# B and C of chunks 4 and 5 before the last w_in quarter, and units 0 and 1 in turn on the first three quarters

## The chip, the cores and the metric

The kernel runs on one core of a Trainium2 chip. A core has a matrix engine (TensorE, PE in the profile), a vector engine (VectorE, DVE), an activation engine (ScalarE, ACT), a general engine (GpSimd, POOL) and a queue engine that issues most DMAs (SyncE, SP). Each takes its instructions in the order in which they are written, and waits at the first one whose operands are not there. The metric is device time in microseconds, the median of the runs. Lower is better.

## The reference

A selective state-space layer, followed by a feed-forward layer with gelu. Sizes: 4 batches, 8 heads, 768 positions, head size 32, state size 16; then 3072 tokens of width 256 through 2048 and back.

```python
x, a, B, C = ...                       # x (4,8,768,32), a (4,8,768), B and C (4,8,768,16)
for c in range(nc):                    # chunks of 32
    la = log(clip(a, 1e-6, 1))[chunk]; cum = cumsum(la)
    M = (C @ B^T) * exp(cum_i - cum_j) * causal
    y = M @ x + (C @ state) * exp(cum)
    state = exp(sum(la)) * state + sum_j B_j x_j exp(cum_last - cum_j)
h = y.reshape(3072, 256) @ w_in        # w_in (256, 2048)
out = gelu_tanh(h) @ w_out             # w_out (2048, 256), out float32
```

## The kernel before

The positions are cut into chunks of 128, six to a batch, 24 in all. Two chunks make a unit, so units 0 to 2 are batch 0, 3 to 5 batch 1 and so on. Decays are products of `a`, found by one scan per batch on VectorE; B is multiplied by the decay product of its position and C divided by it, so that no mask of exponentials is needed.

The steps of a unit `u`, by the names used in the program, are these. `G.u` is the Gram product of C and B on TensorE, into two pairs of PSUM banks, `ga` and `gb`. `M.u.0` and `M.u.1` multiply it with the causal mask on VectorE, once for `ga` and once for `gb`. `D.u` gives the state sums of its two chunks; `S.u.k` adds one to the running state on VectorE, and `SP.c` spreads the state of chunk `c` over the heads. `Y.u` multiplies mask product and spread state with x and C on TensorE (`Yi` and `YI` for units 4 and up, two units together), and `yev.u` copies the result to `xm`, the input of the feed-forward layer. `s1.u.i` is a part of `xm @ w_in` into one PSUM bank, `gelu.u.i` reads that bank on ScalarE, `s2.u.k.q` is a quarter of `gelu @ w_out` for chunk `2u + k`, `oev` copies the sum out and `store` writes it. For units 0 to 3, `s1` has eight parts of four matmuls of 256 columns, and a part needs w_in's quarter `i // 2`; `s2` has four quarters per chunk, each four matmuls of 256 columns. So a part of `s1` and a quarter of `s2` are the same amount of work on TensorE.

Batch 0 is treated apart, so that work starts early. Its first four chunks have loads of their own (`load_bc0`, `load_x4`), and a scan over the first 128 positions (`clipq`, `Rq`). Chunks 4 and 5 (unit 2) have others: `load_bc1` brings their B and C, `load_a` brings all of `a`, and `clip`, `R`, `tp2`, `recip1` on VectorE give their decays; `mul1`, `T1`, `bh1`, `ce1`, `N1`, `bn1` turn B and C for them, and `pe`, `pp`, `pend` find the decays of whole chunks. Batch 1 is turned on TensorE (`mul`, `T`, `E`, `N`, `bn`, `F`), batches 2 and 3 through DRAM: `load_wr` writes the products, `load_tr` and `load_bn` read them back turned. `G.6`, the first of batch 2, waits for these.

The weights come as four quarters of w_in (`load_wi`, 512 KB each) and four of w_out (`load_wo`), in float32, and are cast to bfloat16 in halves by `wi.q.k` and `wo.q.k`, mostly on GpSimd. `load_x.u` and `castx.u` do the same for x from unit 2 on.

There are four single PSUM banks, `bank_a`, `bank_b`, `bank_o` and `bank_y`. A step takes a bank by default (`s1` and `D` take a and b in turn, `s2` takes o, `Y` takes y), or the one named behind an `@` in the table. Before the first work TensorE multiplies zeros into `bank_y`: `~47` means 47 blocks of 128 columns of that filler.

The order of everything is written out by hand: the string `ORDERED` lists the steps, and each is issued when its name comes. `name:A`, `:D`, `:P` or `:S` puts it on another engine than its default one. An engine therefore sees its own steps in the order of the list, and every wait is on data, on a buffer or on a bank. DMAs rotate through eight completion semaphores, so a DMA is issued when the eighth one before it has landed.

Of the kernel before, what the change touches and what calls it, by code (L numbers as in the profile page):

```python
# [21 lines left out]
load_wi.2 SP.0 ~13 Y.0 wi.0.1:A wi.0.0:A S.0.0 clip R S.0.1 yev.0.0.2 wi.1.1 XX.1 XD.1 wi.1.0 tp2 wi.2.1
xn.2 s1.0.0 G.1 S.1.0 s1.0.1 xn.3 gelu.0.0 gelu.0.1 s1.0.2 gelu.0.2 M.1.1 wi.2.0 M.1.0 s1.0.3 gelu.0.3
s1.0.4 s1.0.5 recip1 S.1.1 gelu.0.4 gelu.0.5 SP.1 load_wi.3 wi.3.1 wi.3.0 load_bc1.1 s1.0.6 load_bc1.0
mul1.0:P SP.2 pe mul1.1:P T1.0 bh1:D tp6 Y.1 gelu.0.6 pp load_wo.0 pend:D yev.1.0.2 T1.1 N1 wo.0.0 s1.0.7
load_x.2 ce1.1:D castx.2.None ce1.0:D recip.1 s1.1.0 bn1 SP.3 gelu.0.7 wo.0.1 G.2 D.2 gelu.1.0 S.2.0
s1.1.1 gelu.1.1 s2.0.0.0 s1.1.2 gelu.1.2 s1.1.3 load_bc.1.1 SP.4 load_bc.1.0 M.2.1 M.2.0 gelu.1.3
load_wo.1 s2.0.1.0 mul.1.0 s1.1.4 hold.4 mul.1.1:P recip.2 load_x.3 gelu.1.4 wo.1.0 s1.1.5 wo.1.1 Y.2
gelu.1.5 castx.3.None s1.1.6 yev.2.0.2 T.1.0 s1.1.7 gelu.1.6 load_wo.2 E.1.0 T.1.1 s1.2.0 N.1 gelu.1.7
# [1053 lines left out]
```

## Time and profile before

| | |
|---|---|
| median of 3 runs | 116.78 us (116.25 to 117.2) |
| the profiled execution, its span | 116.7 us |
| TensorE busy (matmuls) | 107.8 us, 92% |
| VectorE, ScalarE, GpSimd busy | 66.2, 69.8, 24.8 us |
| granted TensorE clock | full in all 40 slices |
| DMA | 15.99 MB, 137 GB/s over the span |
| longest wait of TensorE on another engine after the start | 1.3 us, for the casts of w_in |

The page of a profile gives no other time of its execution than the span, from the first to the last instruction. In the lines shown below, L and a number is the line of the kernel; L790 is `s1` of units 0 to 3, L816 `s2`, L644 and L637 `G`, L679 `D`, L701 and L710 `Y`, L721 `Yi`, L654 `M`, L752 `S`, L759 `SP`, L801 `gelu`. Lines 348, 350 and 352 are a copy or cast on ScalarE, GpSimd and VectorE, whatever the step. A line of the order in time is start, length, engine, line, operation, tiles and count; in square brackets stands how long the engine had been idle, and what ended that.

### The profile page before, as it was taken

To read this page: it belongs to the slowest core of one execution; us is meant where nothing else is said; L and a number is where in the kernel's file an instruction comes from. 1 tells how busy PE (TensorE), PEld (TensorE's weight loads), DVE (VectorE), ACT (ScalarE), POOL (GpSimd) and SP (SyncE) were. 2 spreads that over 40 slices of the span, in tenths; PEclk is the share of its full clock that TensorE was granted. 3 is DMA by queue.
4 is the path that set the end of the run, shared out by engine and by line. 5 is a ranking of instruction groups with operands and counts; after the bars stand their busy time and mean duration, and the time that the engine had idled before them with its cause. 6 is when DMAs were issued, how large, how long until landed. Compare 5 with 4: busy or idle time off the path is not lost.

```text
span 116.7 us, 3120 instructions
## 1 busy us (share of the span) xinstructions
PE 107.8 (92%) x1276; PEld 77.6 (66%) x1284; DVE 66.2 (57%) x136; ACT 69.8 (60%) x135; POOL 24.8 (21%) x53
## 2 busy tenths in 40 slices
PE   6989758799999999999999999999999999999990
PEld 2345547588788969665766775777657676777870
DVE  3799995699899279399806901928614521011010
ACT  4179675587575655469774688834775565763500
POOL 7644737455526400050010200000000000000000
PEclk9999999999999999999999999999999999999999
DMA  0999949996997787895978802220000013301032
GB/s 26 254 313 314 305 81 239 286 230 178 296 249 117 144 168 152 201 248 170 217 145 142 169 3 93 96 90 6 0 0 0 0 51 123 101 0 45 6 135 90
DMA packets 43102, 15.99 MB, mean 137 GB/s; under 512 B 36688, under 2 KB 41552, under 8 KB 43088
## 3 DMA queue, kind: packets, MB, share of 16 engines
q1 hardware_dynamic: 42992, 15.76, 54.9%
q8 instruction: 10, 0.16, 0.7%
q10 hardware_dynamic: 96, 0.03, 0.1%
q14 instruction: 4, 0.03, 0.1%
HBM read 11.07 MB, written 3.93 MB: 129 GB/s over the span
## 4 chain that ended last, share of the span: by engine, by line
PE 52%; SPq 27%; DMA 14%; issue 2%; ACT 2%; DVE 0%; DVEq 0%
PE bank_y L816 13%; PE bank_o L816 12%; SPq L175 10%; PE bank_b L795 8%; SPq L194 7%; PE bank_a L795 6%; DMA wf<-in_moe_w_in_dram 5%; SPq L168 5%; DMA x_t<-in_x_dram 4%; PE bank_o L795 3%; DMA scr<-bc 2%; DMA bn<-scr 2%; PE bank_y L795 2%; PE bank_b L816 2%; PE bank_a L816 1%
## 5 line engine op out<-in xcount | busy, mean ns | idle before, releaser
L816 PEld LDWEIGHTS <-gT 128*128 128x128 bf16 x384 | 37.1, 98 | 10.4 <-issue 0.6
L816 PE MATMUL bank_o<-w_out_sb,gT 128*128 128x256 bf16 x192 | 26.1, 273 | 0.0
L816 PE MATMUL bank_y<-w_out_sb,gT 128*128 128x256 bf16 x160 | 21.2, 273 | 0.1
L795 PEld LDWEIGHTS <-w_in_sb 128*128 128x128 bf16 x128 | 14.2, 114 | 7.5 <-issue 0.4
L804 ACT ACTIVATE gT<-bank_b 128x512 bf16<-128x512 f32 x25 | 14.9, 597 | 6.5 <-PE bank_b L795 6.1
L654 DVE TENSOR_TENSOR m<-ga,tri 128x1024 bf16<-128x1024 f32 x12 | 14.6, 1218 | 5.2 <-PE gb L637 5.2
L804 ACT ACTIVATE gT<-bank_a 128x512 bf16<-128x512 f32 x21 | 12.6, 599 | 6.8 <-PE bank_a L795 2.5
L790 PEld LDWEIGHTS <-w_in_sb 128*128 128x128 bf16 x128 | 13.5, 114 | 4.1 <-POOL w_in_sb L350 1.6
L801 ACT ACTIVATE gT<-bank_b 128x512 bf16<-128x512 f32 x17 | 10.1, 597 | 8.7 <-PE bank_b L790 8.6
L795 PE MATMUL bank_b<-xm,w_in_sb 128*128 128x512 bf16 x48 | 14.5, 380 | 0.2
L654 DVE TENSOR_TENSOR m<-gb,tri 128x1024 bf16<-128x1024 f32 x11 | 13.4, 1216 | 0.0
L790 PE MATMUL bank_b<-xm,w_in_sb 128*128 128x256 bf16 x68 | 10.3, 274 | 1.7 <-POOL w_in_sb L350 1.3
L795 PE MATMUL bank_a<-xm,w_in_sb 128*128 128x512 bf16 x36 | 11.2, 380 | 0.1
L352 DVE COPY o_sb<-bank_y 128x256 f32<-128x256 f32 x5 | 2.1, 425 | 15.7 <-PE bank_y L816 13.7
L801 ACT ACTIVATE gT<-bank_a 128x512 bf16<-128x512 f32 x15 | 8.9, 595 | 3.4 <-PE bank_a L790 3.3
L790 PE MATMUL bank_a<-xm,w_in_sb 128*128 128x256 bf16 x60 | 9.0, 273 | 0.9 <-ACT gT L801 0.4
L759 DVE SCALAR_TENSOR_TENSOR sp_new<-s_new,pend,bmask 128x256 bf16<-128x256 f32 x17 | 8.2, 497 | 0.3 <-DVE s_new L752 0.2
L352 DVE CAST xm<-bank_a 128x512 bf16<-128x512 f32 x4 | 2.8, 692 | 9.7 <-PE bank_a L734 9.7
L773 PE MATMUL bank_y<-wz 128*128 128x512 bf16 (+2 forms) x20 | 7.1, 499 | 1.1 <-DVE warm L225 1.1
L510 POOL TENSOR_TENSOR bc<-bc_t,pt 128x768 bf16<-128x768 f32 x3 | 4.7, 1563 | 14.6 <-PE bank_o L795 11.6
L804 ACT ACTIVATE gT<-bank_o 128x512 bf16<-128x512 f32 x10 | 6.0, 597 | 2.4 <-PE bank_o L795 2.3
L348 ACT ACTIVATE xm<-bank_y 128x512 bf16<-128x512 f32 x8 | 4.8, 596 | 3.8 <-PE bank_a L734 3.5
(149 smaller groups left out, 130.9 us busy)
## 6 DMA issues: line engine op xcount, KB each, us to landing
out_dram<-o_sb SPq DMA_DIRECT2D x24, 128.0 KB, 1.8
x_t<-in_x_dram SPq DMA_DIRECT2D x20, 128.0 KB, 4.3
wf<-in_moe_w_in_dram SPq DMA_DIRECT2D x4, 512.0 KB, 6.4
wf<-in_moe_w_out_dram SPq DMA_DIRECT2D x4, 512.0 KB, 6.5
bc_t<-in_C_dram SPq DMA_DIRECT2D x3, 384.0 KB, 6.9
bc_t<-in_B_dram SPq DMA_DIRECT2D x3, 384.0 KB, 6.3
scr<-bc SPq DMA_DIRECT2D x4, 192.0 KB, 3.0
x_t<-in_x_dram SPq DMA_DIRECT2D x1, 512.0 KB, 5.0
```

The source lines that it names most:

```text
L168: nc.sync.dma_start(out=d["bc"][:, i], in_=(B, C)[i][b].rearrange("h (p r) n -> p h (r n)", r=R6))
L175: (nc.scalar if eng == "ACT" else nc.sync).dma_start(out=XF[u][:, k], in_=x[b, :, (c + k) * Q:(c + k + 1) * Q, :].rearrange("h p d -> p h d"))
L194: nc.sync.dma_start(out=WF[("o", q)], in_=wo[q])
L352: nc.vector.tensor_copy(out=o, in_=i)
L654: nc.vector.tensor_tensor(out=m_of(u)[:, 2 * i:2 * i + 2].rearrange("p g k e t -> p (g k e) t"), in0=gx[i].rearrange("p g (k t) -> p (g k) ...
L759: nc.vector.scalar_tensor_tensor(out=sp_new.rearrange("p (g d) -> p g d", g=4), in0=(XN[0][:, H * D:H * D + 64] if gc == 0 else state[("s" ...
L773: nc.tensor.matmul(out=t[:, 0:m * 128], lhsT=wz, rhs=w3.to_broadcast([128, m, 128]), start=True, stop=True, skip_group_check=True)
L790: nc.tensor.matmul(out=hp[:, j * T:(j + 1) * T], lhsT=w_in_k[:, w, q, k], rhs=xm[:, w, u * T:(u + 1) * T], start=(w == 0), stop=(w == 1))
L795: nc.tensor.matmul(out=hp, lhsT=w_in_k[:, w, q, k], rhs=xm[:, w, u * T:u * T + PT], start=(w == 0), stop=(w == 1))
L801: nc.scalar.activation(gts[u][:, 2 * i:2 * i + 2], hp.rearrange("p (j t) -> p j t", j=2), AF.Gelu_apprx_tanh)
L804: nc.scalar.activation(gts[("p", u)][:, i], hp, AF.Gelu_apprx_tanh)
L816: nc.tensor.matmul(out=ops[gc], lhsT=gts[u][:, fi, k * Q:(k + 1) * Q], rhs=w_out_sb[:, fi, :], start=(fi == 0 and (u > 0 or k == 0)), stop ...
```

## The change

Only the table changes. Three things are moved.

First, the DMA issues on SP's queue, in the stretch from the first w_in quarter to x of unit 4. The order before is this (`bcf_95` is B and C of chunks 4 and 5, `bc_t` those of batch 1, `wf` the weights, `x_t` x of a unit):

```order
L190 DMA wf<-in_moe_w_in_dram 128x2x512
L162 DMA a_t<-in_a_dram 32x256 x3
L162 DMA a_t<-in_a_dram 32x192
L190 DMA wf<-in_moe_w_in_dram 128x2x512 x3
L154 DMA bcf_95<-in_C_dram 128x8x32
L154 DMA bcf_95<-in_B_dram 128x8x32
L194 DMA wf<-in_moe_w_out_dram 128x1024
L175 DMA x_t<-in_x_dram 128x8x32 x2
L168 DMA bc_t<-in_C_dram 128x8x96
L168 DMA bc_t<-in_B_dram 128x8x96
L194 DMA wf<-in_moe_w_out_dram 128x1024
L175 DMA x_t<-in_x_dram 128x8x32 x2
```

The same stretch of SP's queue after the change (line numbers are one higher):

```order
L191 DMA wf<-in_moe_w_in_dram 128x2x512 x3
L163 DMA a_t<-in_a_dram 32x256 x3
L163 DMA a_t<-in_a_dram 32x192
L155 DMA bcf_95<-in_B_dram 128x8x32
L155 DMA bcf_95<-in_C_dram 128x8x32
L191 DMA wf<-in_moe_w_in_dram 128x2x512
L195 DMA wf<-in_moe_w_out_dram 128x1024
L176 DMA x_t<-in_x_dram 128x8x32 x2
L195 DMA wf<-in_moe_w_out_dram 128x1024
L169 DMA bc_t<-in_C_dram 128x8x96
L169 DMA bc_t<-in_B_dram 128x8x96
L195 DMA wf<-in_moe_w_out_dram 128x1024
```

The second and third w_in quarter now stand ahead of `a`, B and C of chunks 4 and 5 ahead of the fourth, and each of the next w_out quarters one place earlier among the small loads.

Second, the parts of `s1`. ScalarE's evictions show it, since each `gelu` reads the bank of one part (`gT`), and `xm` is the eviction of a `Y`. ScalarE before, from unit 0's second x to unit 1's second part:

```order
L348 ACTIVATE x16_393<-bank_o_145 128x256
L801 ACTIVATE gT_395<-bank_b_144 128x2x256
L801 ACTIVATE gT_395<-bank_a_143 128x2x256
L801 ACTIVATE gT_395<-bank_b_144 128x2x256
L801 ACTIVATE gT_395<-bank_a_143 128x2x256
L801 ACTIVATE gT_395<-bank_b_144 128x2x256
L801 ACTIVATE gT_395<-bank_a_143 128x2x256
L801 ACTIVATE gT_395<-bank_b_144 128x2x256
L348 ACTIVATE xm_140<-bank_y_146 128x2x2x128
L348 ACTIVATE bn01_136<-ga_141 128x256
L801 ACTIVATE gT_395<-bank_b_144 128x2x256
L801 ACTIVATE gT_395<-bank_a_143 128x2x256 x2
```

ScalarE after, from the same place to the sixth part of unit 0 and the first four of unit 1:

```order
L349 ACTIVATE x16_395<-bank_o_145 128x256
L802 ACTIVATE gT_403<-bank_b_144 128x2x256
L802 ACTIVATE gT_403<-bank_y_146 128x2x256
L802 ACTIVATE gT_403<-bank_a_143 128x2x256
L802 ACTIVATE gT_403<-bank_o_145 128x2x256
L802 ACTIVATE gT_403<-bank_b_144 128x2x256
L349 ACTIVATE xm_140<-bank_y_146 128x2x2x128
L802 ACTIVATE gT_403<-bank_a_143 128x2x256
L802 ACTIVATE gT_403<-bank_o_145 128x2x256
L802 ACTIVATE gT_403<-bank_b_144 128x2x256
L802 ACTIVATE gT_403<-bank_y_146 128x2x256
L802 ACTIVATE gT_403<-bank_a_143 128x2x256
```

The parts go round all four banks, and behind six parts of unit 0 come four of unit 1, ahead of the two of unit 0 that need the fourth quarter. On TensorE the order is now 0.0 to 0.4, `Y.1`, 0.5, 1.0 to 1.2, `T1.0`, 1.3, `T1.1`, `N1`, 0.6, 0.7, `G.2`, `pp`, 1.4, 1.5, `s2.0.0.0`, `D.2`.

Third, the steps up to `G.5` are newly ordered on every engine. `G.1` comes before `Y.0`; on VectorE `M.1.1` and `M.1.0` come ahead of `clip` and the scan; more `s2` work comes before `G.3`, `G.4` and `G.5`; `D.2` takes bank y and `D.4` bank a; w_out's casts are all on GpSimd, and one half of w_in's fourth quarter on VectorE. The filler before `Y.0` is 4 blocks, not 13. VectorE near unit 5, before (`x_t_776` is x of unit 6, `x_t_773` of unit 5, `m_862` the mask product of unit 4, `m_929` of unit 5):

```order
L654 TENSOR_TENSOR m_862<-gb_142,tri_112 128x1024
L654 TENSOR_TENSOR m_862<-ga_141,tri_112 128x1024
L352 CAST x16_896<-x_t_776 128x512
L352 CAST x16_919<-x_t_773 128x512
L654 TENSOR_TENSOR m_929<-gb_142,tri_112 128x1024
L752 SCALAR_TENSOR_TENSOR s_new_940<-s_new_858,pend_129,bank_a_143 128x64
```

And after (`x_t_808` is x of unit 5, `x_t_811` of unit 6, `m_884` unit 4, `m_941` unit 5):

```order
L655 TENSOR_TENSOR m_884<-gb_142,tri_112 128x1024
L655 TENSOR_TENSOR m_884<-ga_141,tri_112 128x1024
L353 CAST x16_931<-x_t_808 128x512
L655 TENSOR_TENSOR m_941<-gb_142,tri_112 128x1024
L353 CAST x16_943<-x_t_811 128x512
L753 SCALAR_TENSOR_TENSOR s_new_950<-s_new_880,pend_129,bank_a_143 128x64
```

Unit 5's x is cast first, and unit 6's cast stands between the two halves of unit 5's mask product. From `D.5` on, the steps stand in the order of before, but for `s2.2.1.0` to `s2.2.1.2`, which now come ahead of `G.5`. Of the table itself, two pieces of the beginning:

```diff
-c_warm c_sel c_cz c_bmask clipq load_wi.0 load_a.0:S load_a.1:S load_a.2:S load_a.3:S Rq tpq recip0 c_m16
+c_m4 c_warm c_sel c_cz c_bmask clipq load_wi.0 Rq tpq recip0 c_m16 mulc.0 ~47 tw.1 ew.1.1:A mulc.1 tw.2
...
-load_wi.2 SP.0 ~13 Y.0 wi.0.1:A wi.0.0:A S.0.0 clip R S.0.1 yev.0.0.2 wi.1.1 XX.1 XD.1 wi.1.0 tp2 wi.2.1
+xn.1 ME.3 xn.0:D SP.0 S.0.0 ~4 G.1 Y.0 load_bc1.0 load_bc1.1 wi.0.1:A wi.0.0:A yev.0.0.2 M.1.1 XX.1 XD.1
```

93 lines of the change are left out of this document (47 added, 46 removed).

## The prediction

> **What bounds the kernel now.** I read the page's busy shares first, then busy time by stretch, what TensorE waited for, and the order in time of TensorE, VectorE, GpSimd and the DMA issues. First the page, and two stretches:
>
> ```profile
> PE 107.8 (92%) x1276; PEld 77.6 (66%) x1284; DVE 66.2 (57%) x136; ACT 69.8 (60%) x135; POOL 24.8 (21%) x53
> 10.00:22.00 12.00, 8.77 (x163) 6.10 (x160) 9.51 (x27) 8.28 (x17) 6.54 (x12) 1.00 0.90 239
> 60.00:70.00 10.00, 9.75 (x135) 7.05 (x134) 4.92 (x10) 6.25 (x13) 0.62 (x1) 1.00 0.62 119
> ```
>
> After the length of a stretch come TensorE (matmul, weight load), VectorE, ScalarE, GpSimd, granted clock, DMA share and GB/s. From 60 us TensorE is full (9.75 of 10). From 10 to 22 us it is busy 8.77 of 12, the ends of pipelined matmuls included. So the end moves by what the first 22 us give and what the rest doesn't give back. Matmuls of that stretch, in time (start, length), and one piece of the chain of waits:
>
> ```profile
> 12.16 0.60 PE L790 MATMUL bank_b<-xm,w_in_sb 128*128 128x256 bf16 x4 [0.41 <-DVE s_new L752]
> 17.87 0.63 PE L790 MATMUL bank_b<-xm,w_in_sb 128*128 128x256 bf16 x4 [1.31 <-POOL w_in_sb L350]
> 21.91 0.21 PE L679 MATMUL bank_b<-x,bn 128*32 128x64 bf16 x4 [0.73 <-POOL x L350]
> 22.06 0.63 PE L790 MATMUL bank_a<-xm,w_in_sb 128*128 128x256 bf16 x4
> 43.12 1.31 PE bank_y L816 x12
> ```
>
> The last row gives the unit of account: 12 matmuls in 1.31 us, so a group of four (an `s1` step of units 0 to 3, or an `s2` step) holds TensorE 0.437 us. From 12.16 to 22.06 us it did nine groups, 3.9 us of work, beside the small steps. It waits because `s1` alternates between two banks, because all eight groups of unit 0 stand before unit 1, and because the last two of them need the fourth w_in quarter (1.31 us, until 17.87).
>
> **The first 22 us.** GpSimd's casts of the second and third quarter, and what `a` takes ahead of them:
>
> ```profile
> 12.31 1.17 POOL L350 CAST w_in_sb<-wf 128x512 bf16<-128x512 f32 x2 [1.94 <-DMA wf<-in_moe_w_in_dram]
> 13.63 1.18 POOL L350 CAST w_in_sb<-wf 128x512 bf16<-128x512 f32 x2 [0.16 <-DMA wf<-in_moe_w_in_dram]
> 8.00:10.00 2.00, 1.95 (x54) 1.26 (x47) 1.96 (x4) 1.83 (x5) 1.64 (x8) 1.00 0.95 279
> a_t<-in_a_dram SPq DMA_DIRECT2D x3, 32.0 KB, 4.9
> ```
>
> The four pieces of `a`, about 120 KB, no longer stand ahead of these quarters; at 279 GB/s they are 0.43 us. So I take the casts to end at 13.05 and 14.3. The other bound is landings as now, the second cast then ending at 14.8. `a` lands behind them, by about 13.6. VectorE, ScalarE and their lengths:
>
> ```profile
> 10.42 0.22 DVE L750 COPY s_new<-bank_o 128x64 f32<-128x64 f32 x1
> 13.26 1.22 DVE L654 TENSOR_TENSOR m<-gb,tri 128x1024 bf16<-128x1024 f32 x1
> 15.79 0.87 DVE L759 SCALAR_TENSOR_TENSOR sp_new<-s_new,pendq,bmask 128x256 bf16<-128x256 f32 x2
> 10.75 0.29 DVE L362 TENSOR_SCALAR ac<-a_t 128x256 f32<-128x256 f32 x1
> 11.14 0.69 DVE L365 TENSOR_TENSOR_SCAN r_t<-ac,ends 128x256 f32<-128x256 f32 x1
> 12.04 0.99 DVE L375 STREAM_TRANSPOSE rt<-r_t 32x64 f32<-32x64 f32 x4
> 16.77 0.53 DVE L420 TENSOR_TENSOR pe<-pe,m 128x48 f32<-128x48 f32 x1
> 12.79 0.60 ACT L801 ACTIVATE gT<-bank_b 128x512 bf16<-128x512 f32 x1 [0.21 <-PE bank_b L790]
> 19.35 0.60 ACT L348 ACTIVATE xm<-bank_y 128x512 bf16<-128x512 f32 x1 [0.23 <-PE bank_y L710]
> ```
>
> VectorE: `M.1.1` 1.22 from 10.6, three state sums to 12.6, `M.1.0` to 13.75, `SP.1` and `SP.2` (0.87) to 14.55, then clip, scan and transposes (0.29, 0.69, 0.99) to 16.5. So the clip doesn't wait for `a`. TensorE: groups 0.0 to 0.3 on four banks at 12.16, 12.6, 13.1 and 13.55; 0.4 at 14.35, behind its cast; `Y.1` from 14.8 to 15.4, then 0.5. A gelu starts 0.63 after its group (12.16, 12.79) and lasts 0.60, so gelu 0.4 ends at 15.6, `Y.1`'s eviction (0.60) behind it at 16.1, and unit 1 starts at 16.15 with 1.0, 1.1 and 1.2. `T1.0` at 17.55 (its product on GpSimd follows the transposes), 1.3, `T1.1`, `N1`, then 0.6 and 0.7 until 19.5, `G.2` until 19.9. `pp` waits until 20.25 for `pe` (0.53), which stands behind the two `ce1` on VectorE; 1.4, 1.5, `s2.0.0.0` and `D.2` follow until 22.05. That is 15 groups where 9 stand now: **6 x 0.437 = 2.62 us.** The filler cut from 13 blocks to 4 gains nothing by itself: `Y.0` waits for unit 0's mask products and `SP.0` either way.
>
> **From 22 to 48 us** the steps of VectorE and ScalarE come closer behind TensorE's, and some of that gain goes:
>
> ```profile
> 23.09 1.22 DVE L654 TENSOR_TENSOR m<-gb,tri 128x1024 bf16<-128x1024 f32 x1
> 30.30 0.24 PE L679 MATMUL bank_a<-x,bn 128*32 128x64 bf16 x8
> 31.12 1.22 DVE L654 TENSOR_TENSOR m<-ga,tri 128x1024 bf16<-128x1024 f32 x1
> 34.75 0.24 PE L679 MATMUL bank_b<-x,bn 128*32 128x64 bf16 x8
> 35.67 0.18 DVE L752 SCALAR_TENSOR_TENSOR s_new<-s_new,pend,bank_b 128x64 f32<-128x64 f32 x1
> 41.68 0.28 PE L644 MATMUL ga<-ce,bh 32*128 32x256 bf16 x2
> 42.22 1.22 DVE L654 TENSOR_TENSOR m<-gb,tri 128x1024 bf16<-128x1024 f32 x1
> 44.87 1.22 DVE L654 TENSOR_TENSOR m<-ga,tri 128x1024 bf16<-128x1024 f32 x1
> 46.98 0.29 PE L721 MATMUL bank_y<-m,x 128*32 128x128 bf16 x8
> 47.97 0.29 PE L637 MATMUL ga<-ce,bh 32*64 32x256 bf16 x2
> ```
>
> `Y.2` is reached at 23.9. `D.2` comes when it comes now, so the VectorE product behind it still starts at 23.09; it is `M.2.0` now and ends at 24.3: a wait of 0.2 us. Unit 2's first group waits for `Y.2`'s eviction with one `s2` group as cover: 0.3. `D.3` comes at 32.5 and `M.3.0` 0.82 behind it (30.30, 31.12); `M.3.1` and `SP.6` end at 36.15, and `Y.3` wants that state at 35.85: 0.35. `D.4` at 37.6 writes bank a now, not b, and the second group behind it, `s1.3.1`, wants bank a too. `S.4.1` ended 1.10 after `D.4` began (34.75, 35.67 + 0.18); the group would come 0.6 after: 0.5. The largest is the last. `Gram` of unit 5 comes at 41.9, three groups more done than now, but then 7 groups lie between it and `Yi.4` where 10 lie now (5.3 us, 41.68 to 46.98). VectorE still needs, from `G.5`, 0.54 to `M.5.1`, 2.65 to `M.5.0` (42.22, 44.87), 1.22 for it, and now also the cast of unit 6's x, about 0.35, between them: 4.8 us, so 46.65. `Yi.5` would stand at 45.75: 0.9.
>
> Together 2.25 us of new waits (each of the small ones between 0 and 0.8, the last between 0.4 and 1.2: 0.4 to 4.4 in all, if every end were met together). From `Yi.5` at 46.65 to `G.6` are 0.77 us, so `G.6` (Gram of unit 6) starts at 47.4 where it starts at 47.97 now: **0.55 us earlier.** By the count of groups it is 2.62 + 0.29 (a wait at `D.5` that goes, since unit 5's x is now cast ahead of unit 6's) - 2.25 = 0.66; I take 0.6. Behind `G.6` both orders are alike and TensorE is full, so the profiled execution's 116.7 us become **116.1.** The median of the three runs, 116.78, is 0.08 above that span, and I expect the same of the new one.
>
> **The loads behind it.** `G.6` also needs the transposed B of batch 2, through DRAM, behind everything on SP's queue:
>
> ```profile
> 11.69 4.37 SPq L194 DMA_DIRECT2D wf<-in_moe_w_out_dram  x1
> 44.88 1.23 SPq L531 DMA_TRANSPOSE bh<-scr  x1
> bh<-scr SPq DMA_TRANSPOSE x2, 3.1
> 14.50:16.50 2.00, 1.63 (x12) 1.21 (x11) 2.00 (x5) 1.70 (x4) 0.31 (x1) 1.00 0.26 38
> 25.50:27.50 2.00, 2.00 (x46) 1.65 (x41) 1.73 (x3) 1.64 (x4) 0.52 (x2) 1.00 0.29 44
> ```
>
> It lands at 44.88 + 3.1 = 48.0, just in time now. The bytes ahead of it are the same in both orders. What can change are two holes of 2 us in which DMA ran at 0.26 and 0.29 of its share, the first while SP's issue of w_out took 4.37 us behind the small B and C. Now a w_in and a w_out quarter follow B and C, and w_out quarters stand between the small loads. The holes are worth up to 2 x 2 x 0.72 = 2.9 us; new ones could cost as much. I take half back, 1.4: landing at 46.6, 0.8 ahead of need.
>
> **Rivals.** *The new waits are mostly not there* (0.24). For it: they are differences of replayed times, and TensorE's listed waits after 22 us are a few tenths now. With a third of them `G.6` comes 2.91 - 0.75 = 2.2 us earlier, if the loads do: 114.5; with none, 113.8.
>
> *The transpose still lands at 48.0* (0.15): the holes move instead of closing, and TensorE, early, waits at `G.6`: 116.7.
>
> *The quarters don't come earlier* (0.06), the change not doing what it says: group 0.4 goes at 14.85, 0.5 later, and all to `G.6` with it: 116.6.
>
> *Slower: w_out's casts come late on GpSimd* (0.13). Its queue now holds all of w_out's quarters, of which VectorE and ScalarE took one half each, and the last four halves stand behind `mul.1.1` and a cast of x:
>
> ```profile
> 24.15 1.50 POOL L510 TENSOR_TENSOR bc<-bc_t,pt 128x768 bf16<-128x768 f32 x1 [0.72 <-DMA bc_t<-in_C_dram]
> 27.13 1.17 POOL L350 CAST w_out_sb<-wf 128x512 bf16<-128x512 f32 x2 [1.48 <-DMA wf<-in_moe_w_out_dram]
> 29.93 0.92 POOL L350 CAST w_out_sb<-wf 128x512 bf16<-128x512 f32 x1 [1.07 <-DMA wf<-in_moe_w_out_dram]
> 27.97 0.95 DVE L352 COPY ch<-gb 128x768 bf16<-128x768 bf16 x1
> ```
>
> `mul.1.1` (1.50) can start at about 25.2, when its reciprocal is there; five casts at 0.6 end at 29.7, at 0.92 at 31.3. TensorE wants the last at 31.55. It is slower than before by 1% if they end after 31.55 + 0.6 + 1.17 = 33.3, that is if at 0.92 each `mul.1.1` starts beyond 27.2. Its C landed at 24.15 now and has 0.5 MB more ahead of it; 3 us later would do it, and from 28 the casts end at 34.1, 2.55 late: 116.1 + 2.55 = 118.7. The Trainium skill (SBUF — State Buffer, "Who interferes with whom") speaks for it: VectorE and GpSimd take one shared port pair in turn, and the later one blocks fully. By that, with one VectorE copy of 0.95 us ahead of each cast, the five would end at 34.5, and the time would be 119.0. The trace agrees only in part: the casts at 27.13 took 0.59 each beside such copies out of PSUM, the one at 29.93 took 0.92.
>
> **How the numbers follow.** The forecast (0.42) is 116.1, its own range 115.4 to 116.7. The range of all cases runs from the first rival with a third of the waits to a little over the second: 114.4 to 117.2; outside lie the slower case and the ends of the first. A change of 1% (1.17 us) is about what a measurement of this kernel can tell from none. Faster than 115.6: most of the first rival, 0.21, and a quarter of the forecast, 0.11, together 0.32. Slower than 117.9: 0.13. Within 1%: 0.55.
>
> **What would show it.** In the profile after: casts of the quarters near 11.9 and 13.1; `D.2` near 22 us with 15 groups before it; then waits of some tenths at `Y.2`, `Y.3` and `s1.3.1` and the longest before `Yi.5`, on VectorE's mask product; `G.6` near 47.4. A wait of `G.6` on the transpose shows the second rival; waits on w_out's casts near 31 us show the last. I am wrong at the root if the first 22 us don't hold 15 groups, or if VectorE reaches `M.5.0` a microsecond earlier than I replay it.

## The result, and the profile after

The changed kernel took 119.61 us (119.19 to 120.10, four runs), the kernel before 116.99 beside it: 1.026 times as long, with a 95% interval of 1.020 to 1.032. That is slower, and outside the range I gave (114.4 to 117.2). The profiled execution took 119.74 us with a span of 118.0: 1.7 us lie outside the span. A time below is the median of a kernel's executions within 1.5% of its fastest, and where only one is left, it is given as such; the ratios are not formed from these medians, so a quotient of two medians can differ from them by some tenths of a percent.

The page and the busy time by stretch, after (columns as in the prediction):

```profile
PE 108.6 (92%) x1281; PEld 77.5 (66%) x1281; DVE 69.2 (59%) x135; ACT 69.3 (59%) x135; POOL 25.4 (22%) x54
10.00:22.00 12.00, 9.87 (x171) 7.31 (x171) 10.08 (x24) 9.89 (x20) 7.25 (x12) 1.00 0.86 232
22.00:48.00 26.00, 23.72 (x295) 19.53 (x293) 21.68 (x36) 13.21 (x25) 9.37 (x13) 1.00 0.97 198
60.00:70.00 10.00, 10.00 (x135) 7.04 (x133) 4.92 (x10) 6.72 (x14) 0.62 (x1) 1.00 0.53 102
```

TensorE is full from 60 us, as before. From 22 to 48 us it is busy 23.72 of 26, so it stands idle for 2.28; the prediction expected new waits of 0.2 to 0.9 us each there, 2.25 together. Its waits in order of time, with `D.2` (L680) and `G.6` (L638):

```profile
12.38 0.60 PE L791 MATMUL bank_b<-xm,w_in_sb 128*128 128x256 bf16 x4 [0.35 <-DVE s_new L753]
14.35 0.63 PE L791 MATMUL bank_a<-xm,w_in_sb 128*128 128x256 bf16 x4 [0.93 <-POOL w_in_sb L351]
16.10 0.63 PE L791 MATMUL bank_b<-xm,w_in_sb 128*128 128x256 bf16 x4 [0.69 <-ACT gT L802]
23.25 0.21 PE L680 MATMUL bank_y<-x,bn 128*32 128x64 bf16 x4
25.40 0.60 PE L817 MATMUL bank_o<-w_out_sb,gT 128*128 128x256 bf16 x4 [0.51 <-POOL w_out_sb L351]
27.26 0.60 PE L791 MATMUL bank_b<-xm,w_in_sb 128*128 128x256 bf16 x4 [0.16 <-ACT xm L349]
38.90 0.29 PE L702 MATMUL bank_y<-ce,sp_new 128*32 128x128 bf16 x8 [1.33 <-DVE sp_new L760]
41.20 0.60 PE L791 MATMUL bank_a<-xm,w_in_sb 128*128 128x256 bf16 x4 [0.29 <-DVE s_new L753]
48.58 0.30 PE L722 MATMUL bank_y<-m,x 128*32 128x128 bf16 x8 [0.52 <-ACT o_sb L349]
49.72 0.30 PE L638 MATMUL ga<-ce,bh 32*64 32x256 bf16 x2
```

The third part of unit 0 waits 0.93 us for its quarter of w_in, the fifth 0.69 (the row names a gelu, but that of bank b had ended at 13.62, and the cast of the third quarter ended at 16.04); `Y.3` waits 1.33 us for `SP.6`. `G.6` starts at 49.72 instead of 47.4. What stands behind the first two, and behind `Y.3`: SP's issues, GpSimd's casts and products, and VectorE's `SP.6` alone.

```profile
8.22 0.38 SPq L155 DMA_DIRECT2D bcf<-in_B_dram  x1
10.56 0.38 SPq L155 DMA_DIRECT2D bcf<-in_C_dram  x1
13.08 1.37 SPq L191 DMA_DIRECT2D wf<-in_moe_w_in_dram  x1
13.12 1.17 POOL L351 CAST w_in_sb<-wf 128x512 bf16<-128x512 f32 x2 [2.42 <-DMA wf<-in_moe_w_in_dram]
14.44 1.60 POOL L351 CAST w_in_sb<-wf 128x512 bf16<-128x512 f32 x2
35.60 1.50 POOL L511 TENSOR_TENSOR bc<-bc_t,pt 128x768 bf16<-128x768 f32 x1 [2.07 <-DMA bc_t<-in_C_dram]
37.07 1.49 POOL L511 TENSOR_TENSOR bc<-bc_t,rt 128x768 bf16<-128x768 f32 x1
37.13 1.71 DVE L760 SCALAR_TENSOR_TENSOR sp_new<-s_new,pend,bmask 128x256 bf16<-128x256 f32 x1
```

The casts start at 13.12 and 14.44, not at 11.9 and 13.1. The fourth quarter is issued at 13.08, in the moment in which the second lands. `SP.6`, for which the prediction took 0.48 us, takes 1.71 here: it starts 0.06 us after GpSimd's second product.

**A second look at the kernel before** explains more than the first trace of the change. I ran it unchanged:

> The kernel before, unchanged, for a second look. The changed kernel's times stand 1.7 us above its spans (119.74 against 118.0), while of the kernel before only a span of 116.7 and times of 116.25 to 117.24 are known. If the span leaves out the same 1.7 us in both kernels, this run shows a time near 117.0 over a span near 115.3, and the execution whose trace I predicted from was an untypically long one, with the long DMA issue of w_out (4.37 us) as the suspect: that issue then takes 3.5 us or less here. The rival, that the change adds 1.5 us outside the span, expects a span within 0.3 us of the time.

It took 115.75 us with a span of 114.0. In its order in time, and the stretches:

```profile
6.68 1.54 SPq L190 DMA_DIRECT2D wf<-in_moe_w_in_dram  x3
11.62 2.54 POOL L350 CAST w_in_sb<-wf 128x512 bf16<-128x512 f32 x4 [1.21 <-DMA wf<-in_moe_w_in_dram]
14.44 1.18 POOL L350 CAST w_in_sb<-wf 128x512 bf16<-128x512 f32 x2 [0.28 <-DMA wf<-in_moe_w_in_dram]
19.98 0.21 PE L679 MATMUL bank_b<-x,bn 128*32 128x64 bf16 x4
45.52 0.29 PE L637 MATMUL ga<-ce,bh 32*64 32x256 bf16 x1
10.00:22.00 12.00, 10.41 (x179) 7.84 (x178) 11.57 (x30) 8.96 (x19) 7.99 (x14) 1.00 1.04 282
22.00:48.00 26.00, 25.77 (x381) 21.54 (x379) 21.80 (x38) 16.33 (x31) 7.70 (x9) 1.00 0.92 206
```

The fourth quarter is cast from 14.44, where the execution that I predicted from had it from 16.64 on (the same two casts there):

```profile
16.64 1.18 POOL L350 CAST w_in_sb<-wf 128x512 bf16<-128x512 f32 x2 [1.82 <-DMA wf<-in_moe_w_in_dram]
```

Here TensorE has no wait over 0.5 us from 12 to 22 us: the waits of 1.31 and 0.73 are not there, and `D.2` comes at 19.98 instead of 21.91. So the span leaves out 1.7 us in both kernels (the theory put up), and the execution behind the prediction was an untypically long one: 116.7, where the kernel before showed spans of 113.6 to 115.7 in its comparable runs beside the kernels below, and never one above 116.4 at full clock. The suspect that I named, the long issue of w_out, took 3.05 us here for 4.37.

### The profile page after: what moved, and what is told of

It is laid out like the page before. It is cut to its first block, busy times and chain, and to the rows that moved or that the text cites. A ratio compares the mean times of both kernels' runs of the same rounds, so it can differ in the third digit from the quotient of the medians.

```text
span 118.0 us, 3121 instructions
## 1 busy us (share of the span) xinstructions
PE 108.6 (92%) x1281; PEld 77.5 (66%) x1281; DVE 69.2 (59%) x135; ACT 69.3 (59%) x135; POOL 25.4 (22%) x54
## 4 chain that ended last, share of the span: by engine, by line
PE 67%; DMA 14%; DVE 7%; SPq 6%; issue 2%; POOL 1%; ACT 1%; DVEq 0%
PE bank_o L817 16%; PE bank_y L817 13%; PE bank_b L796 9%; PE bank_a L796 8%; DMA wf<-in_moe_w_in_dram 7%; DMA wf<-in_moe_w_out_dram 7%; PE bank_o L796 4%; PE bank_y L796 3%; DVE m L655 3%; PE bank_b L791 2%; SPq L191 2%; PE bank_a L791 2%; DVE sp_new L760 2%; PE ga L638 2%; PE bank_b L817 1%
## 5 line engine op out<-in xcount | busy, mean ns | idle before, releaser
L805 ACT ACTIVATE gT<-bank_b 128x512 bf16<-128x512 f32 x25 | 14.9, 598 | 6.6 <-PE bank_b L796 6.5
L805 ACT ACTIVATE gT<-bank_a 128x512 bf16<-128x512 f32 x21 | 12.6, 599 | 6.7 <-PE bank_a L796 6.6
L796 PE MATMUL bank_b<-xm,w_in_sb 128*128 128x512 bf16 x50 | 14.9, 380 | 0.0
L802 ACT ACTIVATE gT<-bank_b 128x512 bf16<-128x512 f32 x16 | 9.6, 597 | 7.4 <-PE bank_b L791 7.4
L796 PE MATMUL bank_a<-xm,w_in_sb 128*128 128x512 bf16 x42 | 12.5, 380 | 0.0
L791 PE MATMUL bank_b<-xm,w_in_sb 128*128 128x256 bf16 x64 | 9.7, 273 | 1.2 <-ACT gT L802 0.7
L760 DVE SCALAR_TENSOR_TENSOR sp_new<-s_new,pend,bmask 128x256 bf16<-128x256 f32 x17 | 9.1, 552 | 0.2
L802 ACT ACTIVATE gT<-bank_a 128x512 bf16<-128x512 f32 x11 | 6.6, 598 | 2.9 <-PE bank_a L791 2.9
L774 PE MATMUL bank_y<-wz 128*128 128x512 bf16 (+1 forms) x17 | 7.0, 553 | 1.1 <-DVE warm L226 1.1
L791 PE MATMUL bank_a<-xm,w_in_sb 128*128 128x256 bf16 x44 | 6.7, 274 | 1.2 <-POOL w_in_sb L351 0.9
```

Of the source, the lines that this page charges most:

```text
L760: nc.vector.scalar_tensor_tensor(out=sp_new.rearrange("p (g d) -> p g d", g=4), in0=(XN[0][:, H * D:H * D + 64] if gc == 0 else state[("s" ...
L774: nc.tensor.matmul(out=t[:, 0:m * 128], lhsT=wz, rhs=w3.to_broadcast([128, m, 128]), start=True, stop=True, skip_group_check=True)
L791: nc.tensor.matmul(out=hp[:, j * T:(j + 1) * T], lhsT=w_in_k[:, w, q, k], rhs=xm[:, w, u * T:(u + 1) * T], start=(w == 0), stop=(w == 1))
L796: nc.tensor.matmul(out=hp, lhsT=w_in_k[:, w, q, k], rhs=xm[:, w, u * T:u * T + PT], start=(w == 0), stop=(w == 1))
L802: nc.scalar.activation(gts[u][:, 2 * i:2 * i + 2], hp.rearrange("p (j t) -> p j t", j=2), AF.Gelu_apprx_tanh)
L805: nc.scalar.activation(gts[("p", u)][:, i], hp, AF.Gelu_apprx_tanh)
```

## The experiments

Edits are in the table's own words; "loads" is the order on SP's queue. Each ratio is to the kernel before on the same chip, with its 95% interval.

**1. The spread states first.**

```diff
-G.3 S.3.0 S.3.1 M.3.0 M.3.1 ... SP.6 ... SP.7 Y.3
+G.3 S.3.0 S.3.1 SP.6 SP.7 M.3.0 M.3.1 ... Y.3
```

> The changed kernel, with SP.6 and SP.7 (the spread states of unit 3) ahead of M.3.0 and M.3.1 on VectorE. Theory of contention: the two took 2.10 us because they ran beside GpSimd's products of batch 2 (35.60 to 38.56). Ahead of the mask products they run from 34.7, before GpSimd starts, and take about 0.5 us each; the mask products end near 38.1, and TensorE's wait of 1.33 us for SP.6 becomes one of about 0.5 for the second mask product. G.6 starts 0.8 us earlier than 49.7, and the time is about 118.8. Rival: the two steps are slow for a reason of their own (their operands), then they take 2.1 us there too, Y.3 waits as long for the mask product behind them, and the time stays at 119.6.

118.49 us, 1.020 (1.012 to 1.027). VectorE, GpSimd and TensorE's wait:

```profile
34.24 0.88 DVE L760 SCALAR_TENSOR_TENSOR sp_new<-s_new,pend,bmask 128x256 bf16<-128x256 f32 x2
34.78 1.68 POOL L511 TENSOR_TENSOR bc<-bc_t,pt 128x768 bf16<-128x768 f32 x1 [1.92 <-DVE sp_new L760]
37.43 0.24 PE L711 MATMUL bank_y<-m,x 128*32 128x128 bf16 x4 [0.55 <-DVE m L655]
```

The two take 0.88 us together, and now it is GpSimd's product that is the longer one, 1.68 for 1.49. The wait before `Y.3` falls from 1.33 to 0.55, as expected, and from `D.2` to `G.6` it is 25.68 us instead of 26.47. Contention holds, the rival falls. The trace shows this; the times do not part the two kernels, since their intervals overlap, and part of the gain was not this edit's: `D.2` came at 22.62.

**2. The changed kernel again**, for whether all this recurs.

> The changed kernel, unchanged, for a second look. Theory of contention: SP.6 and SP.7 again take about 2.1 us beside GpSimd's products, and TensorE waits again over 1 us before Y.3. Theory of the late quarters: their casts again start later than 12.3 us, the start in the first look at the kernel before; chance alone would as soon put them before 12.0. Time 1.02 to 1.03 of before.

Its one comparable time was 117.64 us, beside a median of 116.10 for the kernel before, which is 1.013 and below what I expected; the three others, at a mean granted clock of 0.986, took 120.11 to 122.82. Of the rest, half failed too: the wait and the late casts. The two spread states took 2.11 us again, but this time `SP.6` went first, 0.10 us ahead of the second product, took its 0.48, and no wait of TensorE is listed there:

```profile
36.27 0.48 DVE L760 SCALAR_TENSOR_TENSOR sp_new<-s_new,pend,bmask 128x256 bf16<-128x256 f32 x1
36.37 1.73 POOL L511 TENSOR_TENSOR bc<-bc_t,rt 128x768 bf16<-128x768 f32 x1
```

So 1.2 us of the first trace (1.71 - 0.48) hang on which of two instructions starts a tenth of a microsecond sooner: from `D.2` to `G.6` it is 25.32 us here for 26.47. And the quarters' casts started at 11.61 and 13.50, so the late ones of the first look are not the rule. Over all traces, the second quarter's casts start at 12.36 on the mean (11.58 to 13.25, six kernels) where `a` stands behind two or three more quarters, and at 11.71 (11.33 to 12.31, twelve) where it stands ahead of them: later, not earlier, though less is loaded ahead. Why was not settled.

**3. `a` first again**, all else as changed.

```diff
-load_wi.0 ... load_wi.1 load_wi.2 load_a.0:S load_a.1:S load_a.2:S load_a.3:S
+load_wi.0 load_a.0:S load_a.1:S load_a.2:S load_a.3:S ... load_wi.1 load_wi.2
```

> The changed kernel, with the four pieces of a ahead of the second w_in quarter again, as before. Theory of the order: the quarters' casts start late (13.12 and 14.44 us) because three quarters of w_in queued close together hold each other up on one slow DMA engine; with a between them the casts start near 12.3 and 13.6 as in the kernel before, and the third part of unit 0 near 13.5 instead of 14.35, all to D.2 some 0.8 us earlier, time about 118.9. Rival, bytes alone: with 120 KB more ahead of them the casts start 0.4 us later still, and the time is 119.6 to 120. Second rival, chance: the slow engine differs from execution to execution, and the casts of the other kernels run here (which have the changed order of loads) start anywhere between 12.0 and 13.2.

118.28 us, 1.016 (1.011 to 1.021); casts at 11.33 and 12.72, `D.2` at 22.26, the wait before `Y.3` 1.3 us as in the changed kernel. Bytes alone would have made it later; that rival falls. With 2 it can't be told how much of the full 0.010 is the order and how much chance.

**4. Both together.**

> The changed kernel with both: a ahead of the second quarter, and SP.6 and SP.7 ahead of M.3.0. Each alone gave 1.016 and 1.020 of before where the changed kernel gave 1.026. If the two causes are apart, the wait of 1.3 us before Y.3 shrinks to 0.5 and the time is 0.8 us below that of a alone, 1.009 to 1.010 of before. Rival: what Y.3 no longer waits for is waited for right behind it (G.4, Yi.4), and it stays at 1.015.

118.21 us, 1.019 (1.011 to 1.026): neither expectation by its time, since the casts started at 12.00 and 13.53 in the trace. From `D.2` to `G.6` it is 25.21 us where `a` first alone has 26.02, so the 0.8 us before `Y.3` were gained there, and lost ahead of `D.2`.

**5. The old loads behind the new steps, and the new loads behind the old steps.**

> The changed kernel with the whole order of loads of before on SP's queue (a ahead of the second quarter, the fourth quarter ahead of B and C, the second w_out quarter behind B and C of batch 1); nothing else moved. Theory of the loads: the new order of loads is the larger part of the loss. With it undone the casts of the quarters start near 11.6 and 12.9, the fourth quarter lands near 15 and not 18.6, B and C of batch 1 near 21 and 24 and not 25.5 and 26.8; G.6 starts near 47 (49.7 in the changed kernel, 45.5 in the second look at the one before), and the time is about 1.005 of before. The rest, 1.3 us before Y.3, stays. Rival, the steps: the newly ordered steps lose as much behind any loads; then it is no better than with a alone put first, 1.016 of before.

> The kernel before with the changed kernel's order of loads on SP's queue alone, all steps as before. Theory of the loads: the fourth quarter lands near 18.6 where the kernel before has it at 14.4 to 16.6, B and C of batch 1 land 2 to 3 us later, and the old steps wait for both: 2 us or more, 1.02 of before or worse. Rival, the loads are harmless: within 0.5% of before.

Both are slower than the kernel before. The old loads took 119.71 and 121.13 us in their two comparable executions, 1.034 and 1.047 of the 115.74 beside them; the profiled one has the changed kernel's span, 118.0, so that they lose more than the change is not shown. The new loads in the old steps took 120.90, 1.042 (1.035 to 1.048). TensorE with the old loads (the first two rows), and VectorE and TensorE with the new loads in the old steps:

```profile
25.57 0.60 PE L817 MATMUL bank_o<-w_out_sb,gT 128*128 128x256 bf16 x4 [1.52 <-POOL w_out_sb L351]
35.28 0.28 PE L645 MATMUL ga<-ce,bh 32*128 32x256 bf16 x2 [0.83 <-DVE ce L550]
```

```profile
14.01 0.54 DVE L362 TENSOR_SCALAR ac<-a_t 128x256 f32<-128x256 f32 x1 [3.12 <-DMA a_t<-in_a_dram]
15.66 0.60 PE L790 MATMUL bank_b<-xm,w_in_sb 128*128 128x256 bf16 x4 [3.66 <-DVE s_new L752]
```

My theory that the loads are the larger part falls in this form. Each order of steps is laid out for its loads. With the old ones, w_out's second quarter stands behind B and C of batch 1, and the new steps want it first. With the new ones, `clip`, the first on VectorE's queue there, waits 3.12 us for `a`, and the states behind it, for which unit 0 waits, with it. The time is what I expected of the new loads (1.02 or worse), but this wait is not the one I named.

**6. The new head, the old steps behind it** (up to `M.2.0` changed, then what is left in the order of before).

> The changed order up to the first half of unit 2's mask product (M.2.0, about 24 us), and behind it what is left in the order of the kernel before. If the loss lies in the steps of 22 to 48 us as they are newly ordered, D.2 is at about 23.3 with 15 groups done, as in the changed kernel, that is 1.4 us ahead of the kernel before by count of groups, and the time is 115.6 to 116.5. If the loss lies in the head (B and C of batch 1 and w_out later, VectorE late from the start), the old order behind it loses as much, and the time is 118.5 to 119.6.

121.67 us, 1.050 (1.040 to 1.060), above both expectations:

```profile
25.76 0.29 PE L711 MATMUL bank_y<-m,x 128*32 128x128 bf16 x8 [1.27 <-DVE m L655]
29.07 0.82 PE L520 MATMUL ga<-ident,bc 128*128 128x128 bf16 x6 [2.24 <-DVE bc L511]
```

`D.2` is at 23.50 with 15 groups, `G.6` at 51.38. The old steps turn B of batch 1 as soon as it used to land, and wait 2.24 us for its product. So the old steps do worse behind the new head than the new ones. That does not clear the new ones, whose waits are counted further down.

TensorE's clock has a part in the losses of 5 and 6. The row of the granted clock (tenths of full speed, 40 slices of 3.0 us) in the kernel with the new loads in the old steps, and in this one:

```profile
PEclk9999976999999999999999999999999999999999
PEclk9999999998599999999999999999999999999999
```

Behind the wait of 3.66 us the granted clock was 0.50 for three microseconds, and behind the one of 2.24 likewise; a group of four then took 0.85 us for 0.44. Behind the waits of 0.9 to 1.5 us in the other traces it stayed at 1.00, but for one in experiment 7. With mean clocks of 0.986 this is, as an estimate, (1 - 0.986) x 119 = 1.7 us or 1.4% in each of the two traces, so the new loads in the old steps lose by their waits alone about as much as the change does.

**7. The fourth quarter early**: right behind the third, ahead of `a`, B and C.

> The changed kernel with the fourth w_in quarter issued right behind the third, ahead of a, B and C. Theory of the held issue: in the changed order the eighth DMA ahead of the fourth quarter is the second quarter, so its issue waits until that has landed (13.08 where the kernel before issued it at 7.83), with only the small a, B and C in flight meanwhile, and DMA runs at 124 GB/s in that slice. Here it is issued near 5.8, there is no such slice before 16 us, and the second w_out quarter lands 1 us or more earlier than 23.3 to 24.3. a, B and C land near 16.5, about 1 us later, and with them the products for unit 2, so the time can go either way: 1.015 to 1.03 of before. Rival, bytes alone set the landings: the slice dips as much, and w_out lands as late.

118.79 us, 1.023 (1.016 to 1.030). The issue is no longer held:

```profile
3.44 3.08 SPq L191 DMA_DIRECT2D wf<-in_moe_w_in_dram  x4
14.03 1.43 SPq L195 DMA_DIRECT2D wf<-in_moe_w_out_dram  x1
```

Now the first w_out quarter is issued at 14.03, when the third w_in quarter has landed: the hold has moved one load on, since the six small loads still stand between. The rate dips a slice later, to 186 GB/s (124 in the changed kernel). The theory holds for the issue. Whether it gives time by itself, this trace can't tell: behind a wait of 0.97 us its clock was 0.50 from 12.8 to 15.8 us, and `D.2` came at 23.79.

**8. Three banks in the kernel before**: parts 0.0 to 0.7 in banks b, y and a in turn, nothing else. Part 0.7 and unit 1's first part then follow each other in bank a (18.53 us), ahead of the first one's gelu, which so reads the other's numbers; no work is left out, but one wait is.

> The kernel before with only one part of the change: the eight parts of unit 0 go round three banks (b, y, a) and no longer two. If the two banks held TensorE back, the idle times of 0.36 to 0.47 us before each second part in the second look at the kernel before shrink, and G.6 and the end come 0.5 us earlier, 0.995 of before. Rival: they are ScalarE's pace (one gelu of 0.60 us for a part of 0.437 us), and behind them the step that waits for VectorE sets D.2; then the time is that of before within 0.3%.

116.15 us, 0.999 (0.996 to 1.003): more banks alone bring nothing that can be measured. The rival's reason is wrong, though. The sixth part in the second look at the kernel before, and the sixth and seventh here:

```profile
16.05 0.60 PE L790 MATMUL bank_a<-xm,w_in_sb 128*128 128x256 bf16 x4 [0.20 <-ACT gT L801]
14.98 0.60 PE L791 MATMUL bank_a<-xm,w_in_sb 128*128 128x256 bf16 x4
16.00 0.63 PE L791 MATMUL bank_b<-xm,w_in_sb 128*128 128x256 bf16 x4 [0.42 <-POOL w_in_sb L351]
```

With two banks the gelus came in pairs every 1.28 us; with three they follow each other at 0.48, so the pairs were the banks' pace and not ScalarE's. The sixth part starts 1.07 us earlier. Then TensorE waits 0.42 us for the fourth quarter, 0.34 for GpSimd's product and 0.26 for `pe`, and `D.2` is at 20.16 for 19.98: what the banks gave went into waits for loads and other engines, as the second half of the rival has it.

**9. Every wait mended, some of it on another engine.**

```diff
-castx.6.None:D ... castx.7.None:D M.5.0 ... s1.3.7 F.2 oev.4:A
+castx.6.None:P ... castx.7.None:P M.5.0 oev.4:A gelu.3.6 ... s1.3.7 F.2
```

(with `a` and the spread states first, `pe` behind `recip1`, `D.4@b`)

> The changed kernel with a ahead of the second quarter, and every wait of 20 to 49 us that its trace names taken apart where it arises: SP.6 and SP.7 ahead of M.3.0; pe right behind recip1 on VectorE; D.4 on bank b again; the casts of x of units 6 and 7 on GpSimd, which is idle from 38.6 us on, so that M.5.0 is not behind them; oev.4 ahead of gelu.3.6 on ScalarE. Theory of single waits: each was worth what TensorE idled for it beside a alone put first (0.8 of the 1.4 before Y.3, 0.4 for pe, 0.45 at the bank of D.4, 0.87 before Yi.4 and Yi.5), 2.5 us together: G.6 near 45.8, time 0.995 to 1.0 of before. Theory of the chain: D.2 comes 2 us later than in the kernel before (22.3 against 19.98 in its second look) and all that hangs on it is late, so mended waits come back further on: 1.01 of before or more.

Its one comparable time was 121.03 us: worse. TensorE at `D.6`, and what GpSimd did, in an execution of 123.56 us:

```profile
51.35 0.30 PE L680 MATMUL bank_b<-x,bn 128*32 128x64 bf16 x8 [3.31 <-POOL x L351]
49.25 1.49 POOL L511 TENSOR_TENSOR bc<-bc_t,pt 128x768 bf16<-128x768 f32 x1 [11.82 <-DMA bc_t<-in_C_dram]
50.68 1.17 POOL L351 CAST x<-x_t 128x512 bf16<-128x512 f32 x2
```

GpSimd was idle for 11.82 us, but in its queue the product of batch 3 stood ahead of the two casts and waited for its load. An engine that is idle is not free. Behind TensorE's 3.31 us the granted clock was 0.50 for four microseconds. `G.6` itself was at 47.49, 0.8 earlier than with `a` first alone. Neither theory is settled by it.

**10. The same by order alone**, with `a` first and no step on another engine.

```diff
-G.2 M.2.1 pp@y pend:D SP.3 ... s1.1.4@a gelu.1.4
+G.2 M.2.1 ... s1.1.4@a gelu.1.4 pp@y pend:D SP.3
-s1.2.2 gelu.2.2 s2.1.0.1 s1.2.3 gelu.2.3 T.1.0 E.1.0 ... s2.0.0.3 s2.0.1.3 oev.0:A oev.1:A D.3 G.3 S.3.0 S.3.1 M.3.0
+s1.2.2 gelu.2.2 T.1.0 E.1.0 s2.1.0.1 ... D.3 G.3 S.3.0 S.3.1 SP.6 SP.7 M.3.0 M.3.1 s2.0.0.3 s2.0.1.3 oev.0:A oev.1:A
-s1.3.1 ... M.5.1 castx.6.None:D ... castx.7.None:D M.5.0 gelu.3.6 ... oev.4:A
+s1.3.1@y ... M.5.1 M.5.0 castx.6.None:D ... castx.7.None:D oev.4:A gelu.3.6
```

> The changed kernel with a ahead of the second quarter, and the waits of 20 to 49 us mended by order alone, without a step on another engine (the casts put on GpSimd in the earlier try waited there behind its product of batch 3): pp behind part 1.4; T.1, N.1, D.3 and G.3 two groups earlier on TensorE, so that ten groups and not seven stand between G.3 and Y.3 less one; SP.6 and SP.7 ahead of M.3.0; part 3.1 in bank y, so that it isn't behind S.4.1; oev.4 ahead of gelu.3.6; M.5.0 right behind M.5.1, ahead of the casts of x. Theory of single waits: with a alone put first TensorE idled 0.49 at pp, 1.44 before Y.3, 0.45 behind S.4.1 and 0.87 before Yi.4 and Yi.5; with these gone G.6 starts at 45.3 to 46, and the time is 0.988 to 0.998 of before. Theory of the chain: the waits come back at T.1.1, G.3 (for the copies of VectorE) or D.5, G.6 starts past 47, and the time is 1.01 of before.

117.62 us, 1.011 (1.007 to 1.015), with `G.6` at 47.66: by both numbers the theory of the chain (1.01, past 47), though `Y.3`, `pp` and `Yi.5` wait no more and no wait came back at `T.1.1` or `G.3`. `D.2` came late (22.75, the third quarter again), and two waits were of my own making:

```profile
45.35 0.60 PE L791 MATMUL bank_b<-xm,w_in_sb 128*128 128x256 bf16 x4 [0.54 <-DVE s_new L753]
47.12 0.29 PE L722 MATMUL bank_a<-m,x 128*32 128x128 bf16 x8 [0.51 <-ACT gT L802]
```

**11. The fourth quarter early as well**: loads as before up to B and C of chunks 4 and 5 (a, then quarters two to four), with the mended steps and with the changed ones; and `D.2` one group earlier.

> The kernel with the mended waits, and on SP's queue the head of before: the fourth w_in quarter right behind the third, ahead of B and C of chunks 4 and 5; the second w_out quarter stays ahead of B and C of batch 1, as in the changed kernel. The eighth DMA ahead of the fourth quarter is then x of the first chunks (landed near 7.8), so it is issued near 7.9 and lands near 14.3, not 17.7; w_out, x of unit 2 and B and C of batch 1 land 2 us earlier than with the mended waits alone (19.3, 20.6, 24.8). Theory of the held issue: the 1.1% that the mended kernel still loses to before sits in these loads (waits of 0.43 for w_out's cast, D.2 behind x of unit 2 at 22.75), and the time is 0.995 to 1.0 of before. Rival, the steps of the head: D.2 stays behind 22 us because of VectorE, and the time stays at 1.008 to 1.011.

> The changed kernel with that same order of loads and its own steps. Theory of the held issue: as w_out and B and C of batch 1 land 2 us earlier than in the changed kernel, it gains over a alone put first (1.016), to 1.008 to 1.012; the waits before Y.3, behind S.4.1 and before Yi.4 stay. Rival: like the whole old order of loads behind these steps (1.05) it loses on a step that now meets another one, and is slower than 1.016.

> As the one with mended waits and the fourth quarter early, with D.2 one group earlier: the cast of unit 2's x ahead of w_out's first two casts on GpSimd, the first s2 quarter of unit 0 behind D.2. Theory of the chain (what hangs on D.2 sets the later waits): G.6 0.4 us earlier than there. Theory that TensorE's own idle time is all that counts: the same time within 0.3%, since D.2 did not wait.

With the mended steps 117.09 us, 1.005 (1.002 to 1.008); with the changed ones 117.88, 1.013 (1.009 to 1.018); with `D.2` moved 117.32, 1.010 (1.007 to 1.014). The first two say that the mended steps are worth 0.8%, and that the early quarter is worth 0.3% (against `a` alone first) to 0.6% (against the mended steps), which is no more than the intervals. By their times 1.005 lies between its two expectations, and 1.013 just above the theory's 1.012. The third expected a gain or nothing and lost:

```profile
22.52 0.21 PE L680 MATMUL bank_y<-x,bn 128*32 128x64 bf16 x4 [0.43 <-DVE pend L353]
37.54 0.24 PE L711 MATMUL bank_y<-m,x 128*32 128x128 bf16 x4 [0.89 <-DVE m L655]
```

`D.2`, put earlier, waits for VectorE. It stands at 22 us because of VectorE and the loads, and no longer because of TensorE.

**12. The two waits of my own mended**: `D.5` and `S.5.0` between `M.5.1` and `M.5.0`, `Yi.4` in banks y and b, `D.6` in a.

> The kernel with mended waits and the fourth quarter early, with the two waits mended that the mending itself had made (0.70 before the part that takes bank b behind D.5, since S.5.0 had slipped behind M.5.0 on VectorE; 0.62 at Yi.4, whose bank a still held part 3.7): D.5 and S.5.0 between M.5.1 and M.5.0, Yi.4 and Yi.5 in banks y and b, D.6 in bank a. Theory of single waits: 1.1 to 1.3 us come back, G.6 starts near 45.8, the time is 0.994 to 0.997 of before, so that the order beats it by a little. Theory of the chain: VectorE reaches M.5.0 later instead, and the time stays at 1.002 to 1.005.

116.39 us, 1.003 (1.000 to 1.005): no difference to the kernel before that can be told. The last wait that is left is `G.6`'s own:

```profile
46.26 0.29 PE L638 MATMUL ga<-ce,bh 32*64 32x256 bf16 x2 [0.34 <-DVE ce L550]
```

By its time this is again the theory of the chain (1.002 to 1.005) and not that of single waits (0.994 to 0.997): of the 1.1 to 1.3 us that the two waits were to give back, the medians show 0.7 (117.09 to 116.39). Still, the loss can be taken back by order alone, from 2.6% to 0.3%. A gain is not in this order: no version beat the kernel before.

## Why the prediction was wrong

**What bounds: right.** From `G.6` to the end of the span it is 68.7 us in the execution that I predicted from, 68.5 in the second look, 68.3 in the changed kernel and in the last one of the mended. So all of the loss lies ahead of `G.6`.

**The step that failed: "that is 15 groups where 9 stand now: 6 x 0.437 = 2.62 us".** Its two largest parts, 1.31 and 0.73 us, were read from one execution, and are not the kernel's: with the fourth quarter cast from 14.44 they vanish. The kernel before does its nine groups by 19.98 us, so fifteen would do no more than break even at 22.60. The changed kernel had them done by 23.25 in its first trace, between 22.07 and 22.99 in those with `a` first. The banks did hold TensorE, as the prediction says, but in experiment 8 that was worth nothing. The first 22 us held no gain of 2.6 us; 0.5 us (22.60 - 22.07) is the most that any trace showed.

**"The casts to end at 13.05 and 14.3": in this trace wrong, both bounds too.** They ended at 14.3 and 16.0. Why these two were late stays open: in experiment 2 the same order had them end at 12.8 and 14.9. What I left out beside the bytes is what the eight semaphores do to the issues, though the overview of the kernel says it. Six small loads between the quarters use up six of eight, so the fourth quarter, issued by 8.2 us before, was held until 13.08, and all loads behind it came later. The rival for late quarters (116.6) was priced at 0.5 us and given 0.06. The step on `clip` held, in that it didn't wait for `a`, but VectorE came to it late: `M.1.0` ended at 14.43 and not 13.75, and then the two `SP` steps took 1.23 us beside GpSimd's casts, for 0.87:

```profile
14.34 1.23 DVE L760 SCALAR_TENSOR_TENSOR sp_new<-s_new,pendq,bmask 128x256 bf16<-128x256 f32 x2
15.49 0.70 DVE L363 TENSOR_SCALAR ac<-a_t 128x256 f32<-128x256 f32 x1
```

It starts at 15.49 where the prediction has the `SP` steps end at 14.55, and takes 0.70 for 0.29. Late quarters and late decays together make the 1.2 us by which `D.2` missed 22.05; the trace does not part them.

**New waits, forecast 2.25 us from 22 to 48 us.** The rows listed give 2.81 (0.51, 0.16, 1.33, 0.29, 0.52). (By the prediction's own replayed times three of its terms come out otherwise: 24.3 - 23.9 = 0.4 at `Y.2` for 0.2, 36.15 - 35.85 = 0.30 at `Y.3` for 0.35, and with 41.9 + 5.3 - 3 x 0.437 = 45.89 at `Yi.5` 0.76 for 0.9; the sum hardly moves.) Against the second look, taking off its six groups, the stretch from `D.2` to `G.6` grew by 26.47 - (25.54 - 2.62) = 3.55 us; with the 0.65 at `D.2` this is the whole 4.2 us between 45.52 and 49.72. That the steps come closer behind TensorE's and give time back was right, and `s1.3.1` (0.29 for 0.5), unit 2's first group (0.16 for 0.3) and `Yi` (0.52 for 0.9, though for ScalarE's `oev.4` and less for `M.5.0`) were oversized. Undersized was `Y.3`, 1.33 for 0.35: I took `SP.6` at the length of a row in which GpSimd stood still. The rule for it stands in the section that I had cited, the Trainium skill's "SBUF — State Buffer", "Who interferes with whom" (a VectorE instruction with two SBUF inputs contends with a GpSimd one that reads SBUF, for a port pair that is an exclusive lock), and I applied it to w_out's casts alone. The traces agree with it in both directions: 1.71 us when `SP.6` is second by 0.06 us (the first look), 0.48 when it is first by 0.10 (experiment 2), and the product then 1.73 for 1.49.

**From the span to the time.** I set the median 0.08 us above the span; the runs show 1.7 in both kernels. A span of 116.1 would have been a time of 117.8. The near equality of 116.7 and 116.78 was two errors that cancelled: a long execution, and the part outside the span.

**The slower rival**: its side was right, its mechanism was not. `mul.1.1` started at 26.45, short of the 27.2 from which w_out's last casts would come late, and they held nobody. Nor did VectorE's copies out of PSUM hold them, on which the prediction's 34.5 us rests: beside two of these copies (from 30.41 to 32.23) the casts took 0.59 each. What came late was w_out's second quarter (0.51 us). The transposed B, the second rival, was waited for in no trace.

**The chances.** 0.13 for slower was too little for a change in which every step of 12 to 48 us was new, and each new wait is one-sided: an order that fits its loads can only be missed. The runs with half of the change show it, at 1.03 to 1.05.

## What to carry to other kernels

Before an idle time is booked as a gain, see whether it is in a second execution: here 2.04 of 2.62 us were waits for two late loads in one trace, and that trace's span lay above all comparable ones. When steps are moved, look up for each two-operand VectorE step what GpSimd runs at its new place, and for each large load which DMA is the eighth ahead of it. An order of steps and an order of loads are one thing: in experiments 5 and 6, halves of the new one lost as much as the whole of it or more. And a long wait can cost TensorE twice: in the three traces with one of 2.2 us or more, its clock was halved for three to four microseconds behind it.

## What the runs showed that I had not expected

Contention between VectorE and GpSimd looks here like a lock and not like a share, in that the instruction that starts first keeps its length: the same `SP` step took 0.48 or 1.71 us by a start of a tenth of a microsecond, and GpSimd's product 1.73 or 1.49. The two `ce` steps of batch 1, bfloat16 with one tensor operand, took 2.45 us beside two products of GpSimd in the kernel with the old loads (the next rows; the second product ran from 33.48 to 35.02), and 0.74 in the kernel of experiment 10, while mask products, which read PSUM, kept their 1.22 beside such a product.

```profile
32.78 2.45 DVE L550 TENSOR_SCALAR ce<-ch,par 128x768 bf16<-128x768 bf16 x2
31.95 1.50 POOL L511 TENSOR_TENSOR bc<-bc_t,pt 128x768 bf16<-128x768 f32 x1 [0.79 <-DMA bc_t<-in_C_dram]
```

Landing times of the same loads in the same order differ by about a microsecond between executions: casts of the second quarter, with `a` ahead of it, started anywhere from 11.33 to 12.31 us, and the third's anywhere from 12.72 to 13.97. A single trace cannot price a wait for a load.
